# A recurrent-attention stage with k's decay on VectorE, the state's decay on ScalarE, v without padding and fewer cleared rows

## The chip, the cores and the metric

The kernel runs on one core of one Trainium2 chip. The metric is the device time of one execution in microseconds (us), lower is better. The engines are named as the profile names them: PE is TensorE's matmul side and PEld its weight load, DVE is VectorE, ACT is ScalarE, POOL is GpSimd, SP is the engine whose queue starts most DMA transfers.

## The reference

Three stages in a row. The first, which the change touches, is a gated linear recurrence over 768 positions for 4 x 8 heads of width 48; the second sends each token to one of eight experts; the third is a dense feed-forward block.

```
for t in range(768):                                   # per batch (4) and head (8), D = 48
    state = alpha[t][:, None] * state + outer(k[t], v[t])
    y[t]  = q[t] @ state
x = y as (3072 tokens, 384)
routed = x @ w_skip > 0;  e = argmax(x @ w_gate)       # routed tokens:
x += gate * (relu(x @ w1[e]) @ w2[e])                  #   one of 8 experts, 384 -> 1024 -> 384
h = x @ w_in;  out = (h - tanh(h)) @ w_out             # 384 -> 2048 -> 384
```

## The kernel before, in words

The recurrence is computed in chunks of 128 positions. There are 24 units u (6 chunks x 4 batches, `NU` = 24, batch u % 4), and the heads of a unit are laid out as 4 pairs (`NP`) of two heads, each head on 64 partitions of which 48 carry data. Every engine works off its instructions in the order in which the program writes them; that order is written out by hand in `astep(s)`, which runs for s = 0 to 23 and works on several units at once.

For one unit the parts are these. `scanF` and `scanG` run a forward and a backward product of the decays alpha along the chunk on DVE (tiles F and G, 128 x 512), with a small reciprocal between them. `mkqh` and `mkkh` multiply q by F and k by G (tiles qh and kh), and four columns pf give the decay over the whole chunk. `mmA` forms the products of kh and qh on PE (tile pa in PSUM, one buffer), `mask` cuts them to the causal triangle on DVE (am). `trk` transposes kh on PE and `evk` copies it to SBUF on ACT (kt). `mmS` adds the carried state and kt times v in PSUM (pd), and `evst` multiplies that by pf into the state tile `st[u % 4]`. `mmYs` and `mmYa` give the unit's output from the old state and from am (py in PSUM, two buffers); `evx`, `mmX` and `evxa` transpose it into token rows and score it for the router. A step s holds the scans of unit s + 2, mmA, trk, evk, mask and mmS of unit s, mmYs, evst and mmYa of unit s - 1, and evx, mmX and evxa of unit s - 2.

Other work lies in the same steps. At steps 14 and 22 the router's arithmetic for a batch of units runs on DVE (`route1`, `route1b`), and one step later `route3`; from step 15 on two rows of tokens per step are written by `scatter`, an indirect DMA that POOL issues, into a table `xb`, which SP's `rload` at step 21 reads back. Every four steps one weight block of the last stage is loaded and split into two parts (`wsplit`: cs, ca, cs and wl on DVE, cl and a second ca on POOL, lines 155 to 170). At steps 2 to 7 SP writes six blocks of cleared rows (776 KB each) into `xb`. SP loads alpha, q and k of a unit four steps ahead (`aload`, tile it) and v three steps ahead (`vload`, tile vt).

After step 23 come the last routing batch, the experts (mm1, mm2, with DVE splitting the expert weights) and the feed-forward block.

## Time and profile before

| | before |
|---|---|
| median of 3 runs | 770.59 us (768.1 to 770.76) |
| the profiled execution, its own time | 771.64 us |
| its span in the profile | 769.9 us |
| PE busy | 696.4 us, 90% |
| DVE busy | 473.5 us, 62% |
| ACT busy | 280.8 us, 36% |
| POOL busy | 257.2 us, 33% |
| mean granted TensorE clock | 0.974 of full speed |

The shares are means over stages that differ. In the profile's forty equal slices (19.2 us each) DVE stands at 7 to 9 tenths up to about 210 us and falls to 3 or 4 tenths in the second half, while PE is at 9 tenths or more from there on. The steps of the recurrence, which the change touches, lie in the first nine slices (8.5 to 175 us). A time in the text such as 92.8 us is measured from the start of the span; the 1.74 us by which the execution is longer than its span lie around it.

### The profile page before, as it was taken

The numbers are of one execution on the slowest core, as the hardware profiler recorded it, in microseconds if no ns is written. First come the engines' busy times: TensorE is split into PE (matmuls) and PEld (weight loads), VectorE is DVE, ScalarE is ACT, GpSimd is POOL, SyncE is SP. The second block draws the span as 40 slices with busy tenths as digits, with TensorE's granted clock in tenths as the row PEclk, the third lists the DMA queues.
The fourth block names the chain that finished last, engine by engine and source line by source line (L and its number), as shares of the span: only waits on it lengthen the run. The fifth ranks groups of instructions, "written<-read, shape, count | busy, mean of one in ns | idle before, by whom it ended". The sixth has DMA issues, their size and how long they took to land.

```text
span 769.9 us, 11892 instructions
## 1 busy us (share of the span) xinstructions
PE 696.4 (90%) x4707; PEld 635.0 (82%) x4707; DVE 473.5 (62%) x698; ACT 280.8 (36%) x508; POOL 257.2 (33%) x196
## 2 busy tenths in 40 slices
PE   4788878857899998999999999999999999999993
PEld 3677767746798888989888989999989899989993
DVE  7999999883779988983775333433333343434331
ACT  2323313212475655663343333333333332333221
POOL 6687657954536754551430100200020020002002
PEclk9999989989999999999999999999999999999997
DMA  9899746524477876861311101100110020001001
GB/s 270 220 278 277 185 93 184 148 82 145 136 279 244 271 252 215 268 206 71 98 42 42 42 0 42 42 1 0 42 42 1 10 74 1 1 0 42 1 1 44
DMA packets 31598, 84.55 MB, mean 110 GB/s; under 512 B 4437, under 2 KB 12661, under 8 KB 31536
## 3 DMA queue, kind: packets, MB, share of 16 engines
q1 hardware_dynamic: 27440, 71.80, 31.5%
q0 software_dynamic: 4096, 11.92, 4.3%
q8 instruction: 39, 0.64, 0.4%
q14 instruction: 23, 0.19, 0.1%
HBM read 67.02 MB, written 17.43 MB: 110 GB/s over the span
## 4 chain that ended last, share of the span: by engine, by line
issue 47%; DVE 29%; PE 14%; POOL 4%; ACT 2%; DMA 2%; another core or an unknown queue 1%; POOLq 0%; DVEq 0%; ACTq 0%
DVE wl L144 5%; DVE F L196 4%; DVE G L203 4%; PE hp L559 4%; DVE am L231 2%; POOL out_dram L511 2%; DVE wl L170 2%; DVE st L282 1%; DVE hl L564 1%; DVE cs L155 1%; PE y L497 1%; PE pa L226 1%; PE yp L577 1%; DVE ca L156 1%; PE yp L579 1%
## 5 line engine op out<-in xcount | busy, mean ns | idle before, releaser
L471 DVE TENSOR_TENSOR g<-h,g 128x512 f32<-128x512 f32 x96 | 66.3, 691 | 161.4 <-ACT g L469 152.2
L511 POOL DMA_INDIRECT out_dram<-ob,id x24 | 23.4, 977 | 335.4 <-DVE ob L510 308.7
L497 PE MATMUL y<-wh,gl 128*128 128x384 f32 x384 | 131.0, 341 | 3.3 <-DVE gl L475 2.8
L497 PE MATMUL y<-wh,gh 128*128 128x384 f32 x384 | 130.2, 339 | 0.0
L497 PE MATMUL y<-wl,gh 128*128 128x384 f32 x384 | 130.1, 339 | 0.0
L475 DVE TENSOR_TENSOR gl<-g,gh 128x512 fp32r<-128x512 f32 x96 | 78.2, 814 | 65.9 <-ACT gh L473 44.0
L469 ACT ACTIVATE g<-h 128x512 f32<-128x512 f32 x96 | 57.3, 598 | 168.2 <-PE h L463 166.0
L463 PE MATMUL h<-xh,wh 128*128 128x512 f32 x288 | 115.5, 401 | 1.0 <-DVE g L471 1.0
L463 PE MATMUL h<-xl,wh 128*128 128x512 f32 x288 | 113.9, 395 | 0.0
L463 PE MATMUL h<-xh,wl 128*128 128x512 f32 x288 | 113.8, 395 | 0.0
L473 ACT CAST gh<-g 128x512 fp32r<-128x512 f32 x96 | 59.6, 620 | 83.4 <-DVE g L471 83.1
L497 PEld LDWEIGHTS y<-wh,gl 128*128 128x128 f32 x384 | 72.6, 189 | 5.2 <-DVE gl L475 5.1
L497 PEld LDWEIGHTS y<-wl,gh 128*128 128x128 f32 x384 | 72.6, 189 | 4.2
L497 PEld LDWEIGHTS y<-wh,gh 128*128 128x128 f32 x384 | 72.6, 189 | 3.9
L463 PEld LDWEIGHTS h<-xl,wh 128*128 128x128 f32 x288 | 54.3, 189 | 12.5
L559 PE MATMUL hp<-eh,wh 128*128 128x256 f32 x192 | 56.8, 296 | 8.4 <-DVE hl L564 8.0
L141 ACT CAST wh<-raw 128x768 fp32r<-128x768 f32 x64 | 53.4, 835 | 26.6 <-PE yp L579 18.5
L463 PEld LDWEIGHTS h<-xh,wh 128*128 128x128 f32 x288 | 54.3, 188 | 10.6 <-DVE g L471 1.9
L463 PEld LDWEIGHTS h<-xh,wl 128*128 128x128 f32 x288 | 54.5, 189 | 8.6
L144 DVE TENSOR_TENSOR wl<-raw,wh 128x768 fp32r<-128x768 f32 x45 | 61.2, 1360 | 0.0
L559 PE MATMUL hp<-eh,wl 128*128 128x256 f32 x192 | 53.8, 280 | 0.0
L559 PE MATMUL hp<-el,wh 128*128 128x256 f32 x192 | 53.7, 280 | 0.0
(139 smaller groups left out, 1273.3 us busy)
## 6 DMA issues: line engine op xcount, KB each, us to landing
raw<-in_wmoe_dram SPq DMA_DIRECT2D x64, 384.0 KB, 3.6
raw<-in_wff_dram SPq DMA_DIRECT2D x16, 768.0 KB, 4.9
it<-in_att_dram SPq DMA_DIRECT2D x40, 289.5 KB, 7.0
vt<-in_vz_dram SPq DMA_DIRECT2D x24, 256.0 KB, 3.0
xb<-zero SPq DMA_DIRECT2D x6, 776.0 KB, 10.7
rows<-xb SPq DMA_DIRECT2D x6, 776.0 KB, 4.4
xe<-xb SPq DMA_DIRECT2D x8, 388.0 KB, 4.7
it<-in_att_dram SPq DMA_DIRECT2D x2, 772.0 KB, 9.5
```

The source lines that it names most:

```text
L141: A.copy(t_["h"], raw_t[i])
L144: (eng or V).tensor_tensor(t_["l"], raw_t[i], t_["h"].bitcast(F32), ALU.subtract)
L196: V.tensor_tensor_scan(flat(d["F"]), d["it"][:, :NP * C], flat(ind), 0.0, ALU.mult, ALU.add)
L203: V.tensor_tensor_scan(flat(d["G"])[:, ::-1], d["it"][:, 1:NP * C + 1][:, ::-1], flat(d1s[u % 2])[:, ::-1], 0.0, ALU.mult, ALU.add)
L463: T.matmul(hp, *todo.pop(0), start=len(todo) == last, stop=not todo)
L469: A.activation(g, hp, AF.Tanh)
L471: V.tensor_tensor(g, hp, g, ALU.subtract)
L473: A.copy(gh, g)
L475: V.tensor_tensor(gl, g, gh.bitcast(F32), ALU.subtract)
L497: T.matmul(o, g_[:, sl_], w_[:, DM:], start=first and n == 0, stop=last and n == len(todo) - 1)
L511: s_ = nc.gpsimd.indirect_dma_start(out[:, :], bass.IndirectOffsetOnAxis(d["id"][:, a:a + 1], 0), ob, None, bounds_check=N - 1, oob_is_err ...
L559: T.matmul(hp, w_[:, ks], x_[:, k], start=n == 0, stop=n == 3 * KT - 1)
```

## The change

Five edits, all in or ahead of the recurrence:

1. `mkkh` runs on DVE in place of POOL, right behind scanG; pf is split off into `mkpf`, which stays on POOL and is issued right behind `mkqh`.
2. `evst` runs on ACT in place of DVE: four copies out of PSUM (128 x 112 each, one per pair of heads), scaled by a column of pf per partition, in place of two DVE multiplications (64 x 192 each). The tile pd becomes one fixed PSUM tile, cleared once, so that what lies between the two heads' blocks stays zero.
3. `mmYs` and `evst` are issued earlier in a step: mmYs ahead of trk, evst ahead of evk.
4. v is loaded without padding (192 KB per unit, 256 KB before); mmYa writes 48 rows per head, into two fixed PSUM tiles that are cleared once.
5. Four blocks of `xb` are cleared, at steps 6 to 9, in place of six at steps 2 to 7; the row numbers that are read back are capped, so that rows never written are dropped. The router's PSUM tile moves from the buffers of py to those of px.

```diff
     def mkkh(u):
         d = U[u]
         d["kh"] = w2.tile([PR, NP, C], F32, tag="kh", name=f"kh{u}", bufs=3)
-        G.tensor_tensor(d["kh"], d["kk"], d["G"], ALU.mult)
+        V.tensor_tensor(d["kh"], d["kk"], d["G"], ALU.mult)
+
+    def mkpf(u):
+        d = U[u]
         if u < NU - B:
 
             d["pf"] = w2.tile([PR, NP], F32, tag="pf", name=f"pf{u}", bufs=4)
...
-                T.matmul(d["py"][HP * j:HP * j + HP, p], d["vt"][:, 2 * p + j], d["am"][:, j, p],
+                T.matmul(d["py"][HP * j:HP * j + D, p], d["vt"][:, 2 * p + j], d["am"][:, j, p],
                          start=p == 0 and u < B, stop=p == NP - 1)
...
     def evst(u):
         d = U[u]
         if u < NU - B:
-            for j in range(2):
-                r = slice(HP * j, HP * j + HP)
-                V.tensor_tensor(st[u % B][r, :, HP * j:HP * j + D], d["pd"][r],
-                                d["pf"][r].unsqueeze(2).to_broadcast([HP, NP, D]), ALU.mult)
+            for p in range(NP):
+                A.activation(st[u % B][:, p, :HP + D], pd[:, p, :HP + D], AF.Copy, scale=d["pf"][:, p:p + 1])
...
+    pd = psS("pd", 1).rearrange("p (a e) -> p a e", a=NP)
+    V.memset(pd, 0.0)
+
+    pys = [psY(f"py{i}", i).rearrange("p (a t) -> p a t", a=NP) for i in range(2)]
...
-    for s in range(2, 2 + (NS + NIN) // 512):
-        r0 = 512 * (s - 2)
+    for s in range(6, 6 + NS // 512):
+        r0 = 512 * (s - 6)
         at[s].append(lambda r0=r0: nc.sync.dma_start(
             xb[r0:r0 + 512, :].rearrange("(a p) d -> p a d", a=4), zero.unsqueeze(1).to_broadcast([128, 4, RW])))
...
         if ok(s + 2):
             scanF(s + 2)
             mkqh(s + 2)
+            mkpf(s + 2)
+        if ok(s - 1):
+            mmYs(s - 1)
         trk(s)
+        if ok(s - 1):
+            evst(s - 1)
         evk(s)
         if ok(s - 2):
             mmX(s - 2)
             evxa(s - 2)
-        if ok(s - 1):
-            mmYs(s - 1)
         mask(s)
         if ok(s - 1):
-            evst(s - 1)
             mmYa(s - 1)
```

How the instructions stand now is shown at two places. The first is DVE in steps 8 and 9, from one scan F to the next. F and G are the scans, d the reciprocal's output, am the masked products, st the state, cs the split of a weight block; the number behind a name only tells tiles apart. Before:

```order
L196 SCALAR_TENSOR_TENSOR F_720<-it_97,ind 128x512
L197 RECIPROCAL d_0_104<-F_720 128x4
L231 TENSOR_TENSOR am_744<-pa_709,maskT 128x1024
L282 TENSOR_TENSOR st_124<-pd_692,pf_546 64x4x48 x2
L203 SCALAR_TENSOR_TENSOR G_756<-it_97,d_0_104 128x512
L160 TENSOR_SCALAR cs_687<-ca_688 128x768
L196 SCALAR_TENSOR_TENSOR F_795<-it_98,ind 128x512
```

And of the change, at the same place:

```order
L196 SCALAR_TENSOR_TENSOR F_722<-it_97,ind 128x512
L197 RECIPROCAL d_0_104<-F_722 128x4
L234 TENSOR_TENSOR am_751<-pa_711,maskT 128x1024
L203 SCALAR_TENSOR_TENSOR G_761<-it_97,d_0_104 128x512
L214 TENSOR_TENSOR kh_763<-it_97,G_761 128x512
L160 TENSOR_SCALAR cs_689<-ca_690 128x768
L196 SCALAR_TENSOR_TENSOR F_798<-it_98,ind 128x512
```

The two state multiplications have left the place between the mask and the scan G, and one multiplication for kh stands behind that scan, ahead of the weight block's split and the next scan F.

The second place is POOL's queue in steps 4 and 5, around one weight block (cl and ca), from the products of one unit to those of the next. Before:

```order
L209 TENSOR_TENSOR qh_437<-it_97,F_434 128x512
L214 TENSOR_TENSOR kh_468<-it_97,G_466 128x512
L218 TENSOR_TENSOR pf_470<-it_97,F_434 128x4
L166 TENSOR_TENSOR cl_404<-cl_404,cs_402 128x768
L167 TENSOR_TENSOR ca_403<-ca_403,wh_474 128x768
L209 TENSOR_TENSOR qh_509<-it_98,F_506 128x512
L214 TENSOR_TENSOR kh_544<-it_98,G_542 128x512
```

And of the change:

```order
L209 TENSOR_TENSOR qh_439<-it_97,F_436 128x512
L221 TENSOR_TENSOR pf_441<-it_97,F_436 128x4
L166 TENSOR_TENSOR cl_408<-cl_408,cs_406 128x768
L167 TENSOR_TENSOR ca_407<-ca_407,wh_477 128x768
L209 TENSOR_TENSOR qh_510<-it_98,F_507 128x512
```

Every kh is gone from this queue; qh and pf, which both need only F, stand together, and the block's two products follow them directly.

## Rows read from the trace of the kernel before

**Rows 1.** Busy time of each engine in two stretches; number of instructions in brackets.

```profile
core 0: us, PE busy (x) PEld busy (x) DVE busy (x) ACT busy (x) POOL busy (x), PEclk, DMA share, GB/s
39.70:98.30 58.60, 49.41 (x653) 44.82 (x650) 57.53 (x64) 18.50 (x40) 44.73 (x32) 1.00 0.90 237
...
215.50:425.00 209.50, 199.94 (x1265) 186.56 (x1266) 167.28 (x218) 109.46 (x189) 93.70 (x54) 1.00 0.54 177
```

**Rows 2.** Waits, 39.7 to 98.3 us: who on whom, total us, times, longest.

```profile
PE pd L271 <- DVE st L282: 9.2, 9, 1.4
```

**Rows 3.** Groups of DVE, 39.7 to 98.3 us: busy, mean ns, idle before.

```profile
L196 DVE TENSOR_TENSOR_SCAN F<-it,ind 128x512 f32<-128x512 f32 x9 | 18.3, 2036 | 0.0
L203 DVE TENSOR_TENSOR_SCAN G<-it,d 128x512 f32<-128x512 f32 x10 | 16.4, 1640 | 0.3
L231 DVE TENSOR_TENSOR am<-pa,maskT 128x1024 f32<-128x1024 f32 x9 | 11.0, 1225 | 0.3
L282 DVE TENSOR_TENSOR st<-pd,pf 64x192 f32<-64x192 f32 x18 | 6.3, 350 | 0.1
L156 DVE SCALAR_TENSOR_TENSOR ca<-raw,cs 128x768 uint32<-128x768 uint32 x2 | 3.8, 1908 | 0.1
```

**Rows 4.** The scans over all steps: ns least/median/most, first and last start.

```profile
L196 DVE TENSOR_TENSOR_SCAN F<-it,ind x24: 1192/1222/7539, 3.5 to 153.4; 128x512 f32<-128x512 f32 x24
L203 DVE TENSOR_TENSOR_SCAN G<-it,d x24: 1215/1230/2523, 5.0 to 162.4; 128x512 f32<-128x512 f32 x24
```

**Rows 5.** Timeline around two units: start, us, engine, instruction.

```profile
92.59 1.43 POOL L214 TENSOR_TENSOR kh<-it,G 128x512 f32<-128x512 f32 x1 [2.09 <-DVE G L203]
92.81 2.29 DVE L196 TENSOR_TENSOR_SCAN F<-it,ind 128x512 f32<-128x512 f32 x1
93.99 1.12 POOL L218 TENSOR_TENSOR pf<-it,F 128x4 f32<-128x4 f32 x1
...
105.27 1.27 POOL L209 TENSOR_TENSOR qh<-it,F 128x512 f32<-128x512 f32 x1 [3.07 <-issue]
105.37 1.23 DVE L231 TENSOR_TENSOR am<-pa,maskT 128x1024 f32<-128x1024 f32 x1
```

**Rows 6.** Timeline of DVE: two operations with no POOL product beside them.

```profile
141.10 0.96 DVE L156 SCALAR_TENSOR_TENSOR ca<-raw,cs 128x768 uint32<-128x768 uint32 x1
...
194.69 0.69 DVE L475 TENSOR_TENSOR gl<-g,gh 128x512 fp32r<-128x512 f32 x1 [0.69 <-ACT gh L473]
```

**Rows 7.** Groups of POOL, 39.7 to 98.3 us.

```profile
L214 POOL TENSOR_TENSOR kh<-it,G 128x512 f32<-128x512 f32 x9 | 15.2, 1688 | 13.0 <-DVE G L203 13.0
L209 POOL TENSOR_TENSOR qh<-it,F 128x512 f32<-128x512 f32 x8 | 12.0, 1501 | 2.7 <-PE py L240 2.4
L218 POOL TENSOR_TENSOR pf<-it,F 128x4 f32<-128x4 f32 x9 | 7.8, 868 | 0.0
L166 POOL TENSOR_TENSOR cl<-cl,cs 128x768 f32<-128x768 f32 x3 | 5.5, 1820 | 0.0
```

**Rows 8.** Groups of ACT, 39.7 to 98.3 us: copies out of PSUM.

```profile
L303 ACT COPY xr<-px 128x384 f32<-128x384 f32 x9 | 4.3, 480 | 1.9 <-PE px L295 1.9
L304 ACT COPY l<-px 128x36 f32<-128x36 f32 x9 | 1.7, 194 | 0.0
```

**Rows 9.** Timeline of PE: mmYa of one unit.

```profile
95.73 1.09 PE L247 MATMUL py<-am,vt 128*64 128x128 f32 x16
```

**Rows 10.** Timeline of DVE and POOL in steps 15 to 21.

```profile
110.26 2.29 DVE L196 TENSOR_TENSOR_SCAN F<-it,ind 128x512 f32<-128x512 f32 x1
...
122.34 1.23 DVE L231 TENSOR_TENSOR am<-pa,maskT 128x1024 f32<-128x1024 f32 x1
...
148.53 1.23 DVE L231 TENSOR_TENSOR am<-pa,maskT 128x1024 f32<-128x1024 f32 x1 [0.63 <-PE pa L226]
...
153.00 0.53 DVE L160 TENSOR_SCALAR cs<-ca 128x768 uint32<-128x768 uint32 x1
...
156.33 1.82 POOL L166 TENSOR_TENSOR cl<-cl,cs 128x768 f32<-128x768 f32 x1
```

More of the change, by code (lines that the diff above doesn't have):

```diff
@@ L61, in tile_kernel @@
 @with_exitstack
-def tile_kernel(ctx: ExitStack, tc: tile.TileContext, att0, att, vz, wsg, wmoe, wff, out):
+def tile_kernel(ctx: ExitStack, tc: tile.TileContext, att0, att, vt, wsg, wmoe, wff, out):
     nc = tc.nc
@@ L236, in mmYs @@
         d = U[u]
-        d["py"] = psY(f"py{u}", u % 2).rearrange("p (a t) -> p a t", a=NP)
+        d["py"] = pys[u % 2]
         if u >= B:
@@ L266, in mmS @@
         if u < NU - B:
-            d["pd"] = psS(f"pd{u}", 1)[:, :NP * D].rearrange("p (a e) -> p a e", a=NP)
             rs = [slice(HP * j, HP * j + HP) for j in range(2)]
+            es = [slice(HP * j, HP * j + D) for j in range(2)]
             if u >= B:
-                for r in rs:
-                    T.matmul(d["pd"][r], ident[:, r], st[u % B][:, :, r.start:r.start + D], start=True, stop=False)
+                for r, e in zip(rs, es):
+                    T.matmul(pd[r, :, e], ident[:, r], st[u % B][:, :, e], start=True, stop=False)
             for p in range(NP):
-                for j, r in enumerate(rs):
-                    T.matmul(d["pd"][r, p], d["kt"][:, p, r], d["vt"][:, 2 * p + j, :D],
+                for j, (r, e) in enumerate(zip(rs, es)):
+                    T.matmul(pd[r, p, e], d["kt"][:, p, r], d["vt"][:, 2 * p + j],
                              start=p == 0 and u < B, stop=p == NP - 1)
@@ L627, in tile_kernel @@
     mkqh(0)
+    mkpf(0)
     scanG(0)
     mkkh(0)
+    for t_ in pys:
+        V.memset(t_, 0.0)
     G.memset(zero, 0.0)
@@ L652, in tile_kernel @@
     mkqh(1)
+    mkpf(1)
     scanG(1)
@@ L689, in ok, with pX_ @@
             return 0 <= u < NU
-        def py_(name):
-            return psY(name, s % 2)
+        def pX_(name):
+            return ps["T"].tile([128, 512], F32, tag=f"X{s % 2}", name=name)
         if ok(s + 4):
@@ L733, in astep @@
         if c1 is not None:
-            route2(c1, py_)
+            route2(c1, pX_)
     aload(3)
@@ L973, in layout @@
     rows[..., AQ + NP * C:] = pairs(inputs["k"]).reshape(NU, 2, D, NP * C)
-    vz = np.zeros((NU, C, H, HP), f)
-    vz[..., :D] = inputs["v"].reshape(B, H, NC_, C, D).transpose(2, 0, 3, 1, 4).reshape(NU, C, H, D)
+    vt = inputs["v"].reshape(B, H, NC_, C, D).transpose(2, 0, 3, 1, 4).reshape(NU, C, H, D)
     wsg = np.zeros((2, HP, NP, 9), f)
@@ L990, in layout @@
         "att": rows[ITS:],
-        "vz": vz.reshape(NU, 128, H * HP),
+        "vt": vt.reshape(NU, 128, DM),
         "wsg": wsg.reshape(PR, NP, 9),
```

6 lines of the change are left out of this document (3 added, 3 removed).

## The prediction

> **What bounds the kernel now.** I read the busy times by stretch first, to see which engine is full while the changed code runs. Between 39.7 and 98.3 us lie nine steps of the recurrence, s = 5 to 13, so one takes 6.51 us. DVE is busy for 57.53 of the 58.60 us, PE for 49.41, POOL for 44.73 and ACT for 18.50 [rows 1]. DVE is full, and PE would need 49.41 / 9 = 5.49 us a step even if it never waited: that is the floor below which no relief of DVE helps. The waits say the same from PE's side: its one large wait, 9.2 us in nine times, is mmS of a unit on the state multiplication that DVE does behind the mask [rows 2].
>
> Then the groups of DVE, to see what fills it. A mask takes 1.225 us whenever it runs. The scans don't behave so: in this stretch a mean F takes 2.036 us and a mean G 1.640 us [rows 3], while over the whole trace the medians are 1.222 and 1.230 us [rows 4]. The work is the same, so the excess is waiting inside the instruction. The timeline shows for what: F begins at 92.81 and lasts 2.29 us while POOL's kh runs from 92.59 to 94.02, that is 1.21 us of waiting plus a normal scan; pf, four columns wide, then takes 1.12 us because it waits for F. A mask beside qh, a little later, shows nothing of the kind: 1.23 us beside 1.27 us [rows 5]. So DVE and POOL shut each other out when both read SBUF, and the mask, whose large operand is in PSUM, escapes.
>
> How much that costs: F (2.036 - 1.222) x 9 = 7.3 us, G (1.640 - 1.230) x 10 = 4.1 us, and ca, 1.908 us twice [rows 3] against 0.96 us where no product of POOL lies beside it [rows 6], 1.9 us. Together 13.3 us of 58.6, or 1.48 us a step. Without it DVE would need 57.53 - 13.3 = 44.2 us, 4.9 us a step, less than PE's floor.
>
> Behind the recurrence nothing can take up a shift: from 215.5 to 425 us PE is busy for 199.9 of 209.5 us at full clock [rows 1], and that stretch begins when the last unit's tokens are in place. What the recurrence gains, the end gains.
>
> **The change part by part.** *DVE's own work.* Out go two state multiplications a step, 2 x 0.350 = 0.70 us [rows 3]. In comes kh, 128 x 512 from two SBUF tiles. Its nearest row is the same shape on DVE, 0.69 us [rows 6]; the mean of ca at 0.96 us for 768 columns would make it 0.64 by columns. I take 0.65. DVE's own work is then as before, 0.05 us less a step; the gain must come from the waiting.
>
> *POOL's work.* Out goes kh, 1.688 us a step with its waits [rows 7]. It is the operation that F ran into at 92.81 us [rows 5], and it is gone in every step. What is left: qh, now issued when F is done, so that it lies beside the mask, which costs nothing [rows 5]; pf behind it, four columns, against the scan G (0.1 us); and one weight block's cl and ca every four steps, 1.82 us each [rows 7].
>
> I lay out one such block by hand, with the durations above. cs on DVE ends and F follows at once, so cl waits for F (POOL's loss). cl runs beside reciprocal and mask, from 1.25 to 3.05 us after cs; G, ready at 2.6, loses 0.45. G runs, then ca, which came first, then kh: kh loses 1.8. qh, held up by ca, goes ahead of the next F, which loses 1.25. That is 3.5 us per block and four steps, or 0.87 a step, where it was 1.48; with pf 0.97. DVE's step is then 4.9 - 0.05 + 0.97 = 5.8 us. That is above PE's floor, so DVE still sets the pace: 9 x 5.8 = 52.4 us, with the idle 1.1 us kept 53.5. **Nine steps: -5 us.** Bounds: -9.2 if DVE falls under PE's floor, -0.4 if the waiting stays and only the 0.05 us is won.
>
> *The state on ACT.* Four copies of 112 columns. Rows of ACT for 36 and 384 columns are 0.194 and 0.480 us [rows 8]; between them 112 columns give 0.26, four 1.03 us. ACT's busy time rises by 9.3 to 28 of 53 us. In time it is covered by PE: mmYs must be through before st is overwritten, and between mmYs and the mmS that waits for st PE has trk, mmX and mmYa to do, of which mmYa alone is 1.09 us [rows 9]. I cost it at nothing; without that cover it would be up to 1 us a step. What ACT holds up behind it is evk, which mmS needs, also behind mmX and mmYa. PE's wait of 9.2 us [rows 2] goes over to its next late input, the mask that mmA of the next unit needs.
>
> *mmYa with 48 rows per head* streams the same 128 columns for each product; I take nothing. *The clears* at the start lie on DVE where it waits for its first loads; nothing. *Four cleared blocks, later, and v a quarter smaller:* DVE never waited for a load in the nine steps (idle before F is 0.0 [rows 3]) although six blocks were written there and the transfer engines were 0.90 busy [rows 1]; nothing.
>
> *The first 39.7 us* hold one ca collision like that above, and the first steps gain and pay kh: -1 us.
>
> *Steps 14 and 15, router arithmetic.* DVE is full here with work that doesn't change. F at 110.26 takes 2.29 us [rows 10], now 1.22: -1.07. One ca collides as above: -0.95. With 0.05 for each step: -2.1 us.
>
> *Steps 16 to 19,* from mask to mask 148.53 - 122.34 = 26.2 us [rows 10], one weight block in them and POOL's row writes on top. At 5.8 us a step 23.2, with some 0.2 for the row writes: -2.8 us. The floor of PE would make it -4.2.
>
> *Steps 20 to 22.* What ends last here is POOL's queue, since the table's rows are read back only when the last rows of step 20 are written, and these stand behind cl and ca. DVE's cs is done at 153.53, but cl begins at 156.33 [rows 10]: qh and kh stand ahead of it. From the mask at 148.53 that is 7.8 us. Now it is mask 1.22, G 1.23, kh 0.65 and cs 0.53, with the step to POOL some 3.8 us if POOL is not behind, 6.5 if it is by one qh. -4.0 or -1.3; I take -3.5, since six kh have left POOL's queue by then.
>
> Sum: -1 - 5 - 2.1 - 2.8 - 3.5 = -14.4 us. The profiled execution took 771.64 us, of which the span is 769.9; 771.64 - 14.4 = 757.2. It stood 1.05 us above the median of the runs, so I expect a median of **756 us**.
>
> **The rivals.**
>
> *PE becomes the bound (the gain is larger).* If kh and F lose less than my layout says, steps run at PE's 5.49 us: -9.2 in the nine steps, -4.2 in 16 to 19, -2 at the start, -3 in 14 and 15, -6 in 20 to 22, sum -24: 747 us. For it: POOL has a third less to do. Against it: cl and ca stay.
>
> *The port is no freer.* POOL keeps qh, pf, cl, ca and the row writes, and kh on DVE is a third operation that reads two SBUF tiles, where the state multiplication read PSUM. If kh is shut out as F was (0.81 us in the mean), a step costs 4.9 - 0.05 + 0.81 and 0.8 more for F and G, 6.46 us: nothing is won in the regular steps, some 3 us in 14 to 22: 768 us. Here the Trainium skill speaks against the change: "SBUF — State Buffer", section "Who interferes with whom", says that a VectorE instruction with two SBUF inputs contends with a GpSimd instruction that reads SBUF, that one with at most one SBUF input does not, and that whoever issues first keeps the other out for a whole instruction. By that rule an instruction that can't be shut out is replaced by one that can. The trace agrees on both halves (2.29 us beside 1.23 us [rows 5]).
>
> *Slower: kh is shut out for several POOL instructions in a row.* One F lasted 7.539 us [rows 4]; it stood through qh, kh, cl and ca one after the other, 6.3 us of waiting. kh stands just where cl, ca and the row writes begin, five times in the run. The gain of 14.4 us is gone from the third such wait on; with all five it would be 5 x 6.3 - 14.4 = 17 us more, 788 us. Against it: it happened to one scan of 48, with a POOL that had more to do.
>
> *The loads come late.* Shorter steps ask for data sooner, with transfers at 0.90 busy [rows 1]. It would keep the four steps with cleared blocks near their old length: -14.4 + 4 x 0.7 = -11.6: 759 us.
>
> **How the numbers follow.** Forecast 0.55, PE as bound 0.17, port no freer 0.16, loads late 0.05, slower by shut-outs 0.07. A change under 0.5%, 3.9 us, can't be told from none. Faster by more than that: the forecast, PE's bound, late loads and a third of "no freer", 0.82; within it 0.11; slower 0.07. The range of 8 in 10 reaches from 747, the sum of the lower bounds, to 768, which takes in "no freer" and leaves out the shut-outs.
>
> **What would show it.** Right: mean F near 1.4 us and G near 1.5 in the nine steps; kh 0.65 to 0.7 on DVE in steps without a weight block; a step of 5.6 to 6 us; PE's wait on st gone; cl in step 20 less than 5 us behind the mask. Wrong: kh at 1.4 us or more in the mean, scans as long as before, or a PE that waits for ACT's st. If the recurrence ends 14 us earlier and the run doesn't, the shift was lost in the passage to the experts, between 172 and 215 us.

## The result, and the profile after

The changed kernel takes 749.34 us in the median of 4 runs (748.99 to 751.63), the kernel before 770.13 us in 4 runs beside them: a ratio of 0.9741, 95% interval 0.9714 to 0.9768. The forecast was 756 us, with a range of 747 to 768. The profiled execution took 751.63 us, its span is 749.8 us.

Where the time came from is read off marks that both traces have: the start of mmA, the mask, the first product of the experts (hp) and the end. The unit's number is in brackets.

| stretch | before, us | after, us | shorter by | forecast |
|---|---|---|---|---|
| start to mmA(5) | 39.71 | 36.15 | 3.56 | 1.0 |
| nine steps, mmA(5) to mmA(14) | 58.57 | 51.11 | 7.46 | 5.0 |
| mmA(14) to mask(16) | 24.06 | 21.75 | 2.31 | 2.1 |
| mask(16) to mask(20) | 26.19 | 24.73 | 1.46 | 2.8 |
| mask(20) to mmA(23) | 23.41 | 20.72 | 2.69 | 3.5 |
| mmA(23) to hp | 40.91 | 35.59 | 5.32 | 0 |
| hp to the end | 557.05 | 559.75 | -2.70 | 0 |

Up to mmA(23) the run is 17.48 us ahead where 14.4 were forecast; then the passage to the experts gives 5.3 us more that were not forecast, and the experts give half of that back. What they give back lies in the first ten us behind hp. PE stands there for 1.83 us (0.37 before) until hl is done, one of the two parts into which hp is split: ACT makes hh, DVE makes hl from it, and ahead of hh in ACT's queue a cast had waited 2.10 us for a weight load. Behind that stand the granted clock of TensorE is 0.71 from 194.16 to 197 us and 0.56 to 199 us (1 is 2.4 GHz, the lower level, 0.5, is 1.2 GHz); before, the same products ran at 1.00.

Busy time of the nine steps (columns as in [rows 1], which this line answers):

```profile
core 0: us, PE busy (x) PEld busy (x) DVE busy (x) ACT busy (x) POOL busy (x), PEclk, DMA share, GB/s
36.15:87.26 51.11, 47.78 (x649) 44.78 (x649) 50.42 (x55) 28.43 (x76) 34.10 (x23) 1.00 0.98 253
```

DVE is still full, 50.42 of 51.11 us, but PE now is busy for 47.78 of them, and the transfers' share has gone from 0.90 to 0.98. The granted clock is 1.00 in this stretch of both kernels, so none of the 7.46 us is the clock's. The groups of DVE, POOL and ACT in the nine steps (they answer [rows 3, 7, 8]):

```profile
L203 DVE TENSOR_TENSOR_SCAN G<-it,d 128x512 f32<-128x512 f32 x10 | 13.1, 1312 | 0.0
L196 DVE TENSOR_TENSOR_SCAN F<-it,ind 128x512 f32<-128x512 f32 x9 | 13.1, 1455 | 0.0
L234 DVE TENSOR_TENSOR am<-pa,maskT 128x1024 f32<-128x1024 f32 x9 | 10.8, 1194 | 0.0
L214 DVE TENSOR_TENSOR kh<-it,G 128x512 f32<-128x512 f32 x9 | 9.1, 1010 | 0.3
L156 DVE SCALAR_TENSOR_TENSOR ca<-raw,cs 128x768 uint32<-128x768 uint32 x2 | 1.9, 960 | 0.1
...
L167 POOL TENSOR_TENSOR ca<-ca,wh 128x768 f32<-128x768 f32 x3 | 8.2, 2730 | 0.0
L166 POOL TENSOR_TENSOR cl<-cl,cs 128x768 f32<-128x768 f32 x3 | 7.8, 2591 | 4.1 <-ACT st L284 4.1
...
L284 ACT ACTIVATE st<-pd,pf 128x112 f32<-128x112 f32 x36 | 9.9, 355 | 18.0 <-PE py L243 18.0
```

F has gone from 2036 to 1455 ns in the mean, G from 1640 to 1312, ca from 1908 to 960; the mask, which never waited, is where it was (1194 and 1225). kh has 1010 ns in the mean. Over all steps (least/median/most, as in [rows 4]) one sees that the waits are now few, and none is longer than one product of POOL:

```profile
L196 DVE TENSOR_TENSOR_SCAN F<-it,ind x24: 1207/1218/2332, 3.6 to 138.1; 128x512 f32<-128x512 f32 x24
...
L203 DVE TENSOR_TENSOR_SCAN G<-it,d x24: 1211/1252/2203, 5.1 to 140.6; 128x512 f32<-128x512 f32 x24
L214 DVE TENSOR_TENSOR kh<-it,G x24: 691/693/2124, 7.3 to 142.1; 128x512 f32<-128x512 f32 x24
```

The longest F lasted 7539 ns before and 2332 now. Where what is left comes from stands in the timeline of one step with a weight block (start, us, engine, instruction):

```profile
60.73 0.56 DVE L160 TENSOR_SCALAR cs<-ca 128x768 uint32<-128x768 uint32 x1
...
61.45 2.58 POOL L166 TENSOR_TENSOR cl<-cl,cs 128x768 f32<-128x768 f32 x1 [1.37 <-ACT st L284]
...
62.55 1.20 DVE L234 TENSOR_TENSOR am<-pa,maskT 128x1024 f32<-128x1024 f32 x1
...
63.66 1.46 DVE L203 TENSOR_TENSOR_SCAN G<-it,d 128x512 f32<-128x512 f32 x1
...
63.99 2.73 POOL L167 TENSOR_TENSOR ca<-ca,wh 128x768 f32<-128x768 f32 x1
...
65.15 2.12 DVE L214 TENSOR_TENSOR kh<-it,G 128x512 f32<-128x512 f32 x1
...
66.68 1.72 POOL L209 TENSOR_TENSOR qh<-it,F 128x512 f32<-128x512 f32 x1
...
67.19 2.28 DVE L196 TENSOR_TENSOR_SCAN F<-it,ind 128x512 f32<-128x512 f32 x1
...
69.61 1.19 DVE L234 TENSOR_TENSOR am<-pa,maskT 128x1024 f32<-128x1024 f32 x1
69.61 1.27 POOL L209 TENSOR_TENSOR qh<-it,F 128x512 f32<-128x512 f32 x1
...
70.95 1.16 PE L229 MATMUL pa<-qh,kh 64*128 64x128 f32 x16 [1.26 <-POOL qh L209]
```

This is the order that the forecast laid out by hand: G loses to cl, kh to ca, F to the qh that ca held up. Against medians of 1.22, 0.69 and 1.22 us they lose 0.24, 1.43 and 1.06 us, 2.7 us in a block where the layout said 3.5. POOL pays as well: cl begins while F runs and ca while G does, and they take 2.6 and 2.7 us here against 1.82 in the kernel before [rows 7].

The waits of the nine steps (who on whom, total us, times, longest) have lost the line of [rows 2]: PE no longer waits for st, and ACT has time to wait for PE:

```profile
ACT st L284 <- PE py L243: 18.0, 9, 3.1
...
PE pa L229 <- POOL qh L209: 4.9, 5, 1.6
```

PE's 4.9 us are put down to qh, which ends last by the profile. In the timeline above the mask ends at 70.80 and mmA starts at 70.95, qh ends at 70.88: both come together. The 4.1 us that the profile puts down to st, of POOL before cl, can't be st's: cl reads no tile of the state, and in the block above it begins at 61.45, behind the cs that it does read (60.73 + 0.56 us).

In step 20 the chain of work that ended last runs over POOL and two transfers (start, us, what):

```profile
140.93 2.72 POOL ca L167
145.40 2.80 DMA xb<-xr,loc
148.21 4.25 DMA rows<-xb
```

cl begins at 138.40, 4.66 us behind mask(20), where it was 7.8 us [rows 10]. But the last two row writes of the first batch stand behind cl and ca, the read of the rows behind them, and PE stands for 7.54 us, until 152.51, before it can transpose those rows and go on to mmA(23). In the kernel before the read went out at

```profile
166.51 0.38 SPq L428 DMA_DIRECT2D rows<-xb  x1
```

that is 17.98 us behind mask(20); now it is 14.47 us. From the read to mmA(23) it takes 6.25 us and took 5.43. The difference lies in the work behind PE's stand, which runs at the lower clock (PEclk is the last column but two):

```profile
152.50:154.46 1.96, 1.95 (x15) 1.56 (x15) 0.62 (x2) 0.48 (x1) 0.00 (x0) 0.50 0.00 0
```

The first three transposes take 0.90 us there, 0.55 before, at a clock of 1.00.

### The profile page after: what moved, and what is told of

It reads as the page before. It is cut to its first block, busy times and chain, and to the rows that moved or that the text cites. A ratio compares the mean times of both kernels' runs of the same rounds, so it can differ in the third digit from the quotient of the medians.

```text
span 749.8 us, 11944 instructions
## 1 busy us (share of the span) xinstructions
PE 688.7 (92%) x4707; PEld 630.8 (84%) x4707; DVE 459.1 (61%) x685; ACT 303.0 (40%) x588; POOL 231.6 (31%) x172
## 4 chain that ended last, share of the span: by engine, by line
PE 31%; issue 31%; DVE 28%; POOL 4%; DMA 3%; ACT 2%; SPq 0%; POOLq 0%; DVEq 0%; ACTq 0%
PE h L464 11%; PE y L498 10%; DVE wl L144 5%; DVE F L196 4%; PE hp L560 4%; DVE G L203 4%; DVE am L234 3%; DVE wl L170 2%; DVE ca L156 2%; POOL out_dram L512 2%; DVE hl L565 1%; DVE cs L155 1%; PE yp L578 1%; PE yp L580 1%; PE yp L579 1%
## 5 line engine op out<-in xcount | busy, mean ns | idle before, releaser
L229 PE MATMUL pa<-qh,kh 64*128 64x128 f32 x384 | 31.7, 310 | 24.8 <-POOL qh L209 13.0
```

The costliest lines, as they stand in the source:

```text
L229: T.matmul(d["pa"][:, j, p], d["kh"][r, p], d["qh"][r, p], start=p == 0, stop=p == NP - 1)
```

## The experiments

All ratios are to the kernel before on the same chip, with their 95% intervals. From the profiles: the nine steps, the start of mmA(23) and of hp, and the way between these two, which turns out to have two values.

| kernel | nine steps | mmA(23) | hp | mmA(23) to hp | ratio |
|---|---|---|---|---|---|
| before | 58.57 | 171.94 | 212.85 | 40.9 | 1 |
| after | 51.11 | 154.46 | 190.05 | 35.6 | 0.9741 [0.9714, 0.9768] |
| e1, kh on POOL | 53.29 | 162.21 | 208.10 | 45.9 | 0.9890 [0.9861, 0.9919] |
| e2, st on DVE | 56.91 | 168.76 | 214.51 | 45.8 | 0.9986 [0.9965, 1.0007] |
| e3, before and 24 ACT copies | 58.57 | 172.25 | 214.69 | 42.4 | 1.0000 [0.9975, 1.0025] |
| e4, POOL does kh as well | 60.33 | 179.38 | 220.35 | 41.0 | 1.0138 [1.0100, 1.0176] |
| e5, old loads | 52.44 | 155.94 | 191.96 | 36.0 | 0.9814 [0.9793, 0.9835] |
| e6, five blocks' products on DVE | 51.54 | 146.44 | 182.11 | 35.7 | 0.9659 [0.9634, 0.9684] |
| e7, mmYs late | 50.26 | 154.35 | 190.25 | 35.9 | 0.9759 [0.9730, 0.9789] |
| e8, before with loads held back | 58.42 | 171.89 | 207.88 | 36.0 | 1.0007 [0.9993, 1.0021] |
| e9, fifth block's products later | 51.13 | 148.82 | 185.61 | 36.8 | 0.9691 [0.9666, 0.9716] |
| e10, e1 with loads held back | 53.31 | 161.77 | 198.68 | 36.9 | 0.9860 [0.9835, 0.9885] |
| e11, e9 and four blocks on DVE | 51.46 | 145.93 | 181.90 | 36.0 | 0.9668 [0.9649, 0.9688] |
| e12, no products | 49.57 | 141.83 | 182.04 | 40.2 | 0.9544 [0.9507, 0.9582] |

Theory A is the forecast's own account: DVE's step is its own work and what it waits while POOL's products keep it out of SBUF. The others are stated where they come up. The profile columns are one execution each. The nine steps are cut at mmA and don't hold a whole number of weight blocks, so where a block is what counts, the text also gives the four steps from mask(6) to mask(10), which hold one: 26.28 us before, 22.93 after.

### Each half of the move undone (e1, e2)

e1 is the changed kernel with kh back on POOL:

```diff
-        V.tensor_tensor(d["kh"], d["kk"], d["G"], ALU.mult)
+        G.tensor_tensor(d["kh"], d["kk"], d["G"], ALU.mult)
```

> The changed kernel with k's product kh back on POOL, all else as changed. Theory A (DVE sets the pace; its step is own work plus waiting at the port it shares with POOL, and the two moves add up): DVE's own work is 4.9 us less 0.70 for the state, the waiting of before (1.48 us) is back, so a step of the stretch s = 5 to 13 takes 5.7 us, as in the changed kernel (5.68), and only steps 15 to 22, where POOL has row writes too, lose 3 to 8 us: 752 to 757 us. Rival B (taking kh off POOL is what brought the gain): steps go back to 6.3 us or more, 763 to 770 us.

e2 is the changed kernel with the state multiplications back on DVE, behind the mask:

```diff
-            for p in range(NP):
-                A.activation(st[u % B][:, p, :HP + D], pd[:, p, :HP + D], AF.Copy, scale=d["pf"][:, p:p + 1])
+            for j in range(2):
+                r, e = slice(HP * j, HP * j + HP), slice(HP * j, HP * j + D)
+                V.tensor_tensor(st[u % B][r, :, e], pd[r, :, e],
+                                d["pf"][r].unsqueeze(2).to_broadcast([HP, NP, D]), ALU.mult)
...
         mask(s)
         if ok(s - 1):
+            evst(s - 1)
             mmYa(s - 1)
```

> The changed kernel with the state's decay back on DVE behind the mask, kh staying on DVE. Theory A: 0.70 us of own work more in each step, DVE still the pace: a step of s = 5 to 13 takes 6.4 us, the run 12 to 15 us more, 761 to 764 us; that is, moving kh alone would have won 5 to 9 us of the 20.8. Rival B (the freed port is the gain): a step stays under 5.9 us and the run under 754 us.

The scans of e1 in its nine steps (mean ns behind the comma):

```profile
L196 DVE TENSOR_TENSOR_SCAN F<-it,ind 128x512 f32<-128x512 f32 x9 | 17.3, 1917 | 0.0
L203 DVE TENSOR_TENSOR_SCAN G<-it,d 128x512 f32<-128x512 f32 x10 | 17.0, 1695 | 0.0
```

and the groups of e2:

```profile
L203 DVE TENSOR_TENSOR_SCAN G<-it,d 128x512 f32<-128x512 f32 x10 | 15.6, 1560 | 0.3
...
L196 DVE TENSOR_TENSOR_SCAN F<-it,ind 128x512 f32<-128x512 f32 x9 | 10.9, 1217 | 0.0
L214 DVE TENSOR_TENSOR kh<-it,G 128x512 f32<-128x512 f32 x9 | 8.0, 889 | 0.3
```

With kh on POOL the scans are as long as before, F 1917 ns against 1455 in the changed kernel; with st on DVE F runs free, G and kh lose 0.3 and 0.2 us in the mean, but st is there again and the step is 6.32 us, as theory A had it (6.4). The step of e1 is 5.92 us, between theory A's 5.7 and rival B's 6.3. The nine steps tell the two apart from each other and from the whole change: 58.57 before, 56.91 with kh moved and st not, 53.29 with st moved and kh not, 51.11 with both (edits 4 and 5 are in all three). There the halves nearly add up, 1.66 + 5.28 against 7.46 us. At mmA(23) e1 stands 7.8 us behind the changed kernel and e2 14.3 us, so behind the nine steps they no longer do. The times that were expected missed: e1 takes 766.4 us where theory A gave 752 to 757, e2 772.8 where it gave 761 to 764. In time neither half brings what the whole does, 0.989 and 0.9986 against 0.9741. In the profiled executions 8.1 and 8.5 us lie in a wait of ACT in the passage; but e10 below takes that wait out of e1 and the time hardly follows. So theory A gives the steps; that the whole is worth more than its halves in time is seen and not explained.

### POOL's kh as a load alone (e4)

Changed kernel; POOL multiplies kh once more into a spare tile that nothing reads:

```diff
         V.tensor_tensor(d["kh"], d["kk"], d["G"], ALU.mult)
+        G.tensor_tensor(spare, d["kk"], d["G"], ALU.mult)
```

> The changed kernel, with POOL forming the product k times G a second time into a tile that nobody reads; the output is unchanged. POOL's load and its reads are as before the change, but no engine waits for that product. Theory A (what POOL's kh cost was the shared port): mean F and G go back to 1.9 and 1.6 us and kh on DVE gets longer; a step of s = 5 to 13 takes 6.4 us or more, the run 763 to 772 us. Rival (POOL's kh cost through the wait for its result): 749 to 753 us.

The groups of DVE in its nine steps:

```profile
L203 DVE TENSOR_TENSOR_SCAN G<-it,d 128x512 f32<-128x512 f32 x10 | 15.2, 1520 | 0.0
L196 DVE TENSOR_TENSOR_SCAN F<-it,ind 128x512 f32<-128x512 f32 x9 | 13.1, 1453 | 0.0
...
L214 DVE TENSOR_TENSOR kh<-it,G 128x512 f32<-128x512 f32 x9 | 9.1, 1010 | 0.3
L160 DVE TENSOR_SCALAR cs<-ca 128x768 uint32<-128x768 uint32 x3 | 4.9, 1640 | 0.0
```

The nine steps take 60.33 us, 9.2 more than without the spare product, and DVE's busy time grows by the same 9.2 us, from 50.42 to 59.64: a product of POOL that nothing waits for costs 1.0 us a step, by its hold on DVE. The time, 783.7 us or 1.4% above the kernel before, is above the 763 to 772 that were expected. And the waiting is not where it was expected: F and kh are as in the changed kernel (1455 and 1010 ns), G goes from 1312 to 1520, and most of it falls on cs and wl of the weight blocks, 553 and 952 ns in the changed kernel and 1640 and 2029 here. cs has only one input in SBUF and is shut out all the same.

### The loads and the clears back (e5)

Changed kernel with v padded to 256 KB a unit and six cleared blocks from step 2 on:

```diff
-    for s in range(6, 6 + NS // 512):
-        r0 = 512 * (s - 6)
+    for s in range(2, 2 + (NS + NIN) // 512):
+        r0 = 512 * (s - 2)
...
-    vt = inputs["v"].reshape(B, H, NC_, C, D).transpose(2, 0, 3, 1, 4).reshape(NU, C, H, D)
+    vt = np.zeros((NU, C, H, HP), f)
+    vt[..., :D] = inputs["v"].reshape(B, H, NC_, C, D).transpose(2, 0, 3, 1, 4).reshape(NU, C, H, D)
```

> The changed kernel with v padded again (256 KB a unit in place of 192 KB) and all the cleared rows written again (six blocks from step 2 on): the decays stay where the change put them. The prediction's view, that the transfers are hidden: mask(5) to mmA(14) as in the changed kernel, mmA(5) at 36 us, and 749 to 751 us. Rival, that the part of the gain that was not forecast (2.6 us before mmA(5), 2.5 us in the nine steps, where the DMA share was 0.98) came from the transfers: mmA(5) back at 38 to 39 us, the nine steps at 52 us or more, and 752 to 755 us.

The profile and the times disagree. In the profile mmA(5) is at 36.06 us, the nine steps lose 1.3 us, hp 1.9 us and the span 0.7 us. In time the ratio is 0.9814 against 0.9741, 5.6 us, and the intervals don't touch. The profiled execution, 752.24 us, is the fastest of four; the others took 754.4 to 754.95, at a granted clock of 0.975 to 0.979 in the mean against 0.982. Beside e7, which is the changed kernel but for an order that costs nothing and ran next to e5, the difference is 3.1 us (754.49 against 751.39). The first stretch owes nothing to the loads, the nine steps 1.3 of their 7.46 us, and these are one wait of DVE for a load, which the changed kernel doesn't have:

```profile
DVE F L196 <- DMA it<-in_att_dram: 1.2, 1, 1.2
```

The transfer edits brought 0.7 us by the profile and 3 to 6 by the times; where the larger figure arises can't be read from the one profile.

### The order within a step (e7)

Changed kernel with mmYs and evst behind mmX and evxa:

```diff
-        if ok(s - 1):
-            mmYs(s - 1)
         trk(s)
-        if ok(s - 1):
-            evst(s - 1)
         evk(s)
         if ok(s - 2):
             mmX(s - 2)
             evxa(s - 2)
+        if ok(s - 1):
+            mmYs(s - 1)
+            evst(s - 1)
```

> The changed kernel with the products with the state (mmYs) and the decayed copies of the state behind the output products (mmX) and their evictions, as the kernel before has them. If the place does not matter because VectorE's step is longer than TensorE's: 749 to 751 us, nine steps 51 us. Rival, that the copies of the state on ScalarE come later by the two evictions (0.48 and 0.19 us) and by the eight products, and TensorE waits for them: 0.5 to 1 us more in a step, nine steps 55 us or more, and 756 to 765 us.

0.9759 against 0.9741, well within both intervals, and the masks agree within 0.12 us from unit 5 on (mmA(5) itself comes 0.8 us later, which makes the nine steps look shorter). The earlier place buys nothing: DVE sets the pace, and ACT's copies of the state have time in either order.

### The split of the weight blocks (e6, e9, e11, e12)

e6 is the changed kernel with cl and ca of the five early weight blocks on DVE:

```diff
+        early = NMU <= i < NMU + NE0
...
-            G.tensor_tensor(t_["f"], t_["f"], t_["s"].bitcast(F32), ALU.mult)
-            G.tensor_tensor(a_, a_, t_["h"].bitcast(F32), ALU.subtract)
+            (V if early else G).tensor_tensor(t_["f"], t_["f"], t_["s"].bitcast(F32), ALU.mult)
+            (V if early else G).tensor_tensor(a_, a_, t_["h"].bitcast(F32), ALU.subtract)
```

> The changed kernel with the two products of each of the five early weight blocks (cl and ca, 128x768) on VectorE in place of GpSimd. Theory A, that VectorE's step is its own work and what it waits behind GpSimd's products: 0.95 us of own work for each of the two, and 2.74 us of waiting given back per block, so 0.8 us less per block; nine steps 50 to 51 us, and 745 to 749 us. Rival, that the waiting stays (it is owed to qh and pf as well) and only the work is added: 1.9 us more per block that lies on the path, nine steps 53 us or more, and 752 to 757 us.

It is faster than expected, 742.0 us, 0.9659, and most of it for another reason. Its groups of DVE in the nine steps:

```profile
L204 DVE TENSOR_TENSOR_SCAN G<-it,d 128x512 f32<-128x512 f32 x10 | 12.5, 1252 | 0.0
L197 DVE TENSOR_TENSOR_SCAN F<-it,ind 128x512 f32<-128x512 f32 x9 | 11.0, 1219 | 0.0
...
L215 DVE TENSOR_TENSOR kh<-it,G 128x512 f32<-128x512 f32 x9 | 6.2, 692 | 0.3
```

All waiting is gone, kh has 692 ns, and yet the nine steps take 51.54 us: three products of each kind, 5.8 us, went into the place of the waiting. That is the cut: the nine steps hold the products of three blocks, but the waiting that they remove belongs to two. From mask(6) to mask(10), one whole block, it is 22.17 us in place of 22.93, the 0.8 us a block of theory A. By mmA(23) the gain is 8.0 us, far more than that. So a new theory E: the passage hangs on the row writes that stand behind the fifth block's cl and ca in POOL's queue. e9 moves nothing to DVE and only issues these two products, and the wl on DVE that needs them, one step later:

```diff
-        for s, f_ in zip((3 - k // 4, 4, 4, 6), wsplit(NMU + k)):
+        for s, f_ in zip((3 - k // 4, 4, 4 + k // 4, 6 + k // 4), wsplit(NMU + k)):
```

> The changed kernel with GpSimd's two products of the fifth early weight block (cl and ca, 5.3 us at 138.40) issued one step later, behind qh(23) and so behind the last two row writes of the first batch; everything else as in the changed kernel. Theory E, that the passage hangs on the row writes: these two writes (143.82 and 145.40) start 5 us earlier, the read of the rows (148.21) goes out at 142 us, TensorE's stand of 7.5 us before the transposes of the rows shrinks to 1 to 2 us, mmA(23) starts at 147 us in place of 154.46, and the time is 742 to 744 us, as with all five blocks' products on VectorE. Rival, theory A for the passage as well: it was the sharing of the port, of which this edit changes nothing, so only part of the 7.4 us comes back: 747 to 750 us.

The timeline of e9 around the read of the rows:

```profile
138.09 0.98 POOL L415 DMA_INDIRECT xb<-xr,loc  x1 [0.30 <-issue]
...
140.71 2.72 POOL L166 TENSOR_TENSOR cl<-cl,cs 128x768 f32<-128x768 f32 x1
140.74 0.38 SPq L429 DMA_DIRECT2D rows<-xb  x1
...
145.81 0.55 PE L437 MATMUL px<-ident,rows 128*128 128x128 f32 x3 [0.86 <-DMA rows<-xb]
...
148.82 2.08 PE L229 MATMUL pa<-qh,kh 64*128 64x128 f32 x16
```

The read goes out at 140.74 in place of 148.21, PE stands 0.86 us in place of 7.54, and mmA(23) starts 5.6 us earlier. E is right in its mechanism. In time it is 745.94 us, 0.9691, 3.9 us under the changed kernel by the ratios and not the 5 to 7 that were expected. e11 adds the products of the first four blocks on DVE:

```diff
+        early = NMU <= i < NMU + NE0 - 1
...
-            G.tensor_tensor(t_["f"], t_["f"], t_["s"].bitcast(F32), ALU.mult)
-            G.tensor_tensor(a_, a_, t_["h"].bitcast(F32), ALU.subtract)
+            (V if early else G).tensor_tensor(t_["f"], t_["f"], t_["s"].bitcast(F32), ALU.mult)
+            (V if early else G).tensor_tensor(a_, a_, t_["h"].bitcast(F32), ALU.subtract)
```

> The fifth block's products one step later on GpSimd, as in the run beside this one, and the products of the first four blocks on VectorE. Theory E: the nine steps stay at 51 to 51.5 us, as they did with all five on VectorE, and the time is that of the run beside this one within 2 us. Rival, theory A: 0.8 us less for each of the four blocks, 3 us less than the run beside this one.

742.91 us, 0.9668 against 0.9691; the intervals overlap, and from e6 it is not told apart. In the profile its nine steps are 0.3 us longer than those of e9, by the same cut as in e6. Cut by blocks, e11 gains 0.8 us on e9 from mask(6) to mask(10) (22.14 against 22.93), as theory A gave, nothing on the third block (28.64 against 28.35 from mask(12) to mask(16), where the router's arithmetic lies), and 1.7 us on the fourth (23.07 against 24.74 from mask(16) to mask(20), among the row writes). At mask(20) it is 2.6 us ahead and at mmA(23) 2.9. So the 3 us of theory A are there in the profile, though unevenly spread.

e12 leaves the ten products out:

```diff
+        early = NMU <= i < NMU + NE0
...
-            G.tensor_tensor(t_["f"], t_["f"], t_["s"].bitcast(F32), ALU.mult)
-            G.tensor_tensor(a_, a_, t_["h"].bitcast(F32), ALU.subtract)
+            if not early:
+                G.tensor_tensor(t_["f"], t_["f"], t_["s"].bitcast(F32), ALU.mult)
+                G.tensor_tensor(a_, a_, t_["h"].bitcast(F32), ALU.subtract)
```

> The changed kernel without the two products (cl and ca) of each of the five early weight blocks; they are left out altogether, so the low halves of these blocks are not the true ones. It measures what these ten products cost on GpSimd. Theory A: what holds VectorE's step above TensorE's is the 2.74 us that G, kh and F wait behind them; without them VectorE needs 22.9 - 2.7 = 20.2 us in four steps, TensorE 4 x 5.28 = 21.1, so every step runs at 5.28 us, the nine steps take 47.5 to 48 us in place of 51.1, mmA(23) starts at 142 to 144 us and the time is 737 to 741 us. Rival: something else (the cs, ca and wl of the block on VectorE, or ScalarE's casts) makes the step with a block longer: the nine steps stay at 50 us or more, and the time is that of the run with the products on VectorE, 742 us, within 2 us.

0.9544. Between 43.6 and 81 us lie seven steps, six of them of 5.28 us. The busy times there:

```profile
43.60:81.00 37.40, 37.04 (x508) 34.76 (x505) 33.29 (x41) 22.23 (x60) 14.58 (x14) 1.00 1.00 256
```

PE is busy for 37.04 of 37.40 us: here it is the bound, at 5.28 us a step. DVE now also stands for the loads of `it`, 3.2 us in two times, at a transfer share of 1.00; PE loses 0.4 us by it, in the last of the seven steps. The nine steps take 49.57 us and not 47.5 to 48, and 1.6 us of the difference lie in the first of them, mmA(5) to mmA(6), which takes 6.92 us: PE had stood for 2.0 us ahead of it and runs it at a clock of 0.70 and then 0.80.

```profile
36.71:40.20 3.49, 3.49 (x28) 3.37 (x29) 3.42 (x6) 1.41 (x4) 1.03 (x2) 0.70 1.04 236
```

The ten products cost 1.5 us in the nine steps (3.2 without that first step's loss) and 12.6 us by mmA(23), so most of what they cost lies behind step 13. The time, 738.8 us, is in the range that theory A gave.

### The stand in the passage (e3, e8, e10)

In the kernel before, the last two evictions of xr on ACT come late. The only input that they have is px, whose products end at 179.94 us by the trace:

```profile
178.80 1.14 PE L295 MATMUL px<-selw,xT 128*128 128x105 f32 x8
...
182.68 0.48 ACT L303 COPY xr<-px 128x384 f32<-128x384 f32 x1 [4.67 <-remote]
...
187.70 0.48 ACT L303 COPY xr<-px 128x384 f32<-128x384 f32 x1 [3.97 <-remote]
```

The profile names nobody of this core for the wait ("remote"). The changed kernel has no such wait; e1 has one of 8.1 us, e2 of 8.5, e3 two as before, e4 one of 5.3, e12 two of together 7.8. It is the two values of "mmA(23) to hp" above: 35.6 to 36.9 us without it, 40.2 to 45.9 with it. Theory C was that ACT waits for its own code; e3 shifts its instructions by 24 in the kernel before:

```diff
     A.activation(warm, warm, AF.Exp)
+    for _ in range(24):
+        A.copy(warm, warm)
```

> The kernel before, with 24 tiny copies on ACT at the very start, where ACT idles for 9 us; nothing else. It moves every later ACT instruction 24 places on in ACT's stream. In the kernel before ACT stands still at 178.0 and at 183.7 us, 4.67 and 3.97 us, for no semaphore that the trace shows, just when a packet of the instruction queues is under way among weight loads; in the changed kernel it does not. Theory C (ACT waits for its own code, and the place where a new piece of the stream begins has moved): both stalls leave that place, the passage from the first row write of the second batch to the first expert weight split gets 4 to 5 us shorter, the run takes 764 to 767 us. Rival (the wait belongs to the data flow): the stalls stay, 769 to 771 us.

The waits stay at the same two evictions (3.97 and 4.66 us) and the time is the same. Nothing speaks for C, but the test is weak: the packets of the two instruction queues, which the shift was to move, still lie beside the stand, at 177.5 and 179.0 us to within half a us, where the kernel before has them at 178.0 and 178.5. What speaks against C is that the changed kernel has such a packet at 162.0 us, as close to the start of the loads (161.92), and no stand. Theory D: the row writes of POOL and the first three loads of expert weights, which start at 177.87 us, are under way together. In the kernel before, the transfers' share and GB/s (last two columns) around the stand are

```profile
180.00:182.00 2.00, 0.89 (x4) 0.38 (x2) 0.00 (x0) 0.00 (x0) 1.67 (x2) 1.00 0.92 374
182.00:184.00 2.00, 0.21 (x1) 0.21 (x2) 0.00 (x0) 1.06 (x3) 1.39 (x3) 0.96 0.97 359
```

e8 (the kernel before) and e10 (e1) hold these loads back by three small copies into their tiles that read the last unit's logits:

```diff
+            if behind is not None:
+                A.copy(raw_t[i][:, :9], behind)
...
     for i in range(RING0):
-        wload(i)
+        wload(i, RT[last]["l4"][:, BATCHES[last] - 1, 0] if i < 3 else None)
```

> The kernel before, with the first three expert weight blocks loaded only behind the last unit's logits (three copies of 9 columns into their tiles on ScalarE hold the loads back); all else as before. Theory D, that TensorE's products in the passage end late because the row writes and the three loads are under way together: ScalarE's waits of 4.67 and 3.97 us before the last two xr fall to about 1.9 and 1.2 us, the first product of the experts (hp) starts 4 to 5 us earlier than 212.85 us, and the time is 765 to 767 us against 770 to 772 of the kernel before. Rival: the row writes alone, or something that has nothing to do with transfers, holds them: the two waits stay above 3.5 us and the time is that of the kernel before, within 2 us.

> The changed kernel with kh on GpSimd (as in the run with that part alone undone, 766.4 us, ScalarE's wait of 8.1 us before the next to last xr) and with the first three expert weight blocks held back behind the last unit's logits. Theory D (the stand is owed to the loads under way beside the row writes, in every execution): the wait falls to about 2 us, hp starts at 202 to 203 us in place of 208.10, and the time falls to 761 to 763 us. Rival, that the stand is there in some executions alone, or is given back among the experts: the profile shows it shorter, and the time stays within 2 us of a ratio of 0.989 to the kernel before.

The two evictions in e8:

```profile
179.92 0.48 ACT L305 COPY xr<-px 128x384 f32<-128x384 f32 x1 [1.97 <-PE px L297]
...
182.21 0.48 ACT L305 COPY xr<-px 128x384 f32<-128x384 f32 x1 [1.23 <-PE px L297]
```

In both profiles the stand is gone: hp starts 5.0 us earlier in e8 and 9.4 in e10 than in the kernel that each is made from. But the times don't follow: e8 has the ratio 1.0007, e10 0.986 against 0.989, which is 2.3 us with intervals that overlap. So the loads have to do with the stand in the profiled executions, as D says, while its rival is right on the time: in the other executions it is either not there or made good later. The changed kernel itself, and e5, e6, e7, e9 and e11 with it, starts the same loads in the middle of its row writes and has no stand, so the loads beside the writes are not the whole cause. That stays open.

## Why the prediction was right, point by point

The median came out 6.7 us under the forecast and 2.3 us above the 747 of the rival with PE as the bound. That it lies in the range is in part luck, since errors cancel: up to step 13 the terms are 5.0 us short, from step 16 on 2.2 us long.

**What bounds the kernel.** DVE was the bound and the waiting was what could be won: the sum of the waits in F, G and ca fell as the scans' means show, and in e4 a product of no use costs DVE as much again, though in cs, wl and G and not in F. That the end gains what the recurrence gains holds within 3 us (17.48 at mmA(23), 20.1 at the end).

**First 39.7 us, forecast -1, measured -3.56.** The step that failed is that I counted one collision of ca there and gave the regular waits of F and G away only from step 5 on. They were there from the second unit: masks 1 to 4 follow each other at 4.32, 4.35 and 6.00 us now, and at 4.45, 4.90 and 6.89 before, 1.6 us together. Another 1.6 us lie between mask(4) and mmA(5): before, mmA(5) came behind mmS, which stood for 2.43 us until st was done; now it follows the mask itself. e5 has mmA(5) at 36.06 too, so the loads have no part in it.

**Nine steps, forecast -5, measured -7.46.** The mechanism was right, instruction by instruction; two sizes were off. The block's waiting was 2.7 and not 3.5 us, and the 0.1 us that G was to lose to pf is not seen (G's median 1.252 us against 1.230 before). kh at 0.69 against 0.65 goes the other way. That gives 5.8 - 0.2 - 0.1 + 0.04 = 5.5 us a step; DVE's busy time is 50.42 / 9 = 5.6. The idle time that I kept, 1.1 us, came down to 0.7. PE's floor of 5.49 was too high for the changed kernel: its step is 5.28 us when it waits for nothing (e12); what makes its busy time in [rows 1] larger was not looked into. By e5 1.3 of the 7.46 us are the transfers', for which the forecast had nothing.

**The port.** The rule of the Trainium skill that the forecast weighed ("SBUF — State Buffer", section "Who interferes with whom": an instruction of VectorE with two SBUF inputs and one of GpSimd that reads SBUF keep each other out) is borne out by kh: 0.69 us alone, 2.12 beside ca. cs has one SBUF input and yet goes from 0.55 to 1.64 us in e4. The same section of the Trainium skill clears an instruction with one SBUF input only outside the modes that use both of VectorE's ports, a condition that the forecast's wording leaves out. That cs runs in such a mode is not shown; it takes 0.72 ns a column where kh takes 1.35 (553 ns for 768 columns, 692 for 512). The rival that it gave, a step of 6.46 us, is not, since kh meets a product of POOL once in a block and not in every step.

**ACT's copies, forecast at no cost.** Four of them span 1.09 us where 1.03 was taken, ACT's busy time rose by 9.9 us as forecast (9.3), and PE no longer waits for st. e7 shows how much room there is: with the copies issued later the time is the same.

**Steps 14 and 15,** -2.1 and -2.31. **Steps 16 to 19,** -2.8 and -1.46: taken at 5.8 us a step they run at 6.18, and e11 and e12, where the products of the blocks have left POOL, take 23.07 and 21.89 us in place of 24.73. The term for the row writes, 0.2 us, was too small, and the trace shows how they cost it: they stand ahead of qh in POOL's queue, so that qh no longer lies beside the mask, where it cost nothing, but beside G, F and kh:

```profile
126.01 1.30 POOL L209 TENSOR_TENSOR qh<-it,F 128x512 f32<-128x512 f32 x1
126.08 2.33 DVE L196 TENSOR_TENSOR_SCAN F<-it,ind 128x512 f32<-128x512 f32 x1
```

A G (120.93) takes 2.17 us beside the qh of 120.72 and a kh (130.90) 1.57 us beside that of 130.52.

**Steps 20 to 22,** -3.5 and -2.69. cl did come less than 5 us behind the mask, and the read of the rows moved with it, by 3.5 us, as forecast. What the forecast left out is what follows the read: PE goes from it to mmA(23) in 6.25 us, 0.8 more than before, at the lower clock behind a longer stand. Nor did I ask what cl and ca ahead of the row writes cost, before and after: 5.6 us by e9. That was in the rows ([rows 10] and POOL's order), and it is more than this whole term.

**Transfers, forecast at nothing.** Off by 0.7 to 1.3 us in the profile of e5 and by 3 to 6 us in its times; if the times are right it is the largest error among the terms. The reason given, that DVE never waited for a load, held for the old pace: at the new one and with the old transfers it waits once, 1.2 us (e5).

**Passage to the experts.** The forecast assumed that the shift is carried; the profile adds 5.3 us, the stand that only the kernel before has, and 2.7 us are given back among the experts. The experiments don't allow crediting the change with the 5.3 us, since taking the stand out of the kernel before (e8) leaves its time as it is.

**The rivals.** PE as the bound (747 us) came close: every second step of the changed kernel takes 5.28 us, but the blocks still hold DVE in the others, as e12 shows by removing their products. Late loads are not the bound of the changed kernel; DVE waits for them in e5 (1.2 us) and in e12, and even there PE sets the step. Several POOL instructions in a row in front of kh did not occur: the longest kh is 2124 ns, the longest F 2332.

A better kernel came out of it: e6, with the five blocks' products on DVE, 742.0 us, 0.9659; e11, 742.9 us, is as good.

## What to carry to other kernels

Where two engines shut each other out, an instruction's own time is its median where nothing lies beside it, and the excess of the mean is what can be won; lay out by hand which instruction stands beside which after the change, as that order gave each wait to within 0.4 us. An operation on an engine that is off the path can cost most of its own time on the path (e4: 1.0 us a step for a product of 1.6), and when its queue also issues transfers, look at what stands in front of those: two products of 2.7 us ahead of a row write cost 5.6 us in the profile here, and issuing them one step later gave back 3.9 us of the time. When an order is laid out by periods, compare whole periods: a stretch cut inside one hid a gain of 0.8 us a block. A mark in a profile that moves (a wait that comes and goes between kernels) is to be tested in the times before it is counted as a gain.

## What the runs showed of the hardware

- ACT's eviction of px began 2.7 us after its products' end by the trace in the kernel before, with transfers at a share of 0.92 to 0.97 and 359 to 374 GB/s. The section "Who interferes with whom" of the Trainium skill's page "SBUF — State Buffer" says that TensorE and ScalarE wait on no other engine at SBUF and that transfers have ports of their own; what was held here, the products' real end, their signal or ACT, no run tells.
- Both sides of a meeting at SBUF pay, whoever comes second: kh grew from 0.69 to 2.12 us beside ca, while cl beside F and ca beside G grew from 1.82 to 2.6 and 2.7 us.
- An operation of DVE with one SBUF input can be shut out too: cs (128 x 768, in 0.55 us) took 1.64 us in e4, where POOL had one product more in each step.
- The granted clock went to its lower level, 1.2 GHz, where TensorE had stood: in the changed kernel it stood from 144.97 to 152.51 us, and the clock is 0.50 from 148 to 157 us; in e12 it stood for 2.0 us, and the clock is 0.70 in the 3.5 us behind. A stand of 1.59 us ahead of mmA(5) in the changed kernel left it at 1.00.
- Narrow copies out of PSUM with a scale per partition take 355 ns each for 112 columns and follow each other at 0.25 us, so four span 1.09 us; a plain copy of 384 columns takes 479 ns.
